# Two half-height PSUM tiles in place of one full-height tile: the first stage of u and the last step of a kernel block

## The chip, the cores and the metric

The kernel runs on one core of one Trainium2 chip. The core has a matmul engine (TensorE, "PE" in the profile, with its weight loads listed as "PEld"), a vector engine (VectorE, DVE), an activation engine (ScalarE, ACT), a general engine (GpSimd, POOL), a queue engine that issues the DMAs (SyncE, SP) and 16 DMA engines. Data lies in SBUF (128 partitions); matmul results go to PSUM, which has eight banks of 128 partitions by 512 float32 numbers. The metric is the time of one execution on the device, in microseconds, smaller being better.

## The reference

Two independent results are put side by side. Left, an S4D state space layer: a long convolution of u with a kernel K made of 256 complex exponentials for each of 448 channels, done with FFTs of twice the length. Right, full softmax attention with 16 heads of 28 over 2048 positions. All numbers are float32.

```python
    def _A_ref(u, log_A_real, A_imag, C_real, C_imag, log_dt, D_skip):
        ...
        A = -jnp.exp(log_A_real) + 1j * A_imag
        C = (C_real + 1j * C_imag) * dt[:, None]
        ...
        P = jnp.exp((A * dt[:, None])[:, :, None] * pos[None, None, :])
        K = 2.0 * jnp.einsum("dn,dnl->dl", C, P).real
        ...
        y = jnp.fft.irfft(Uf * Kf[None, :, :], L2)[:, :, :L]
        ...
        return y + u * D_skip[None, None, :]
    def _B_ref(x, wqkv, wo):
        ...
        scores = jnp.einsum("bhqd,bhkd->bhqk", q, k) * scale
        p = _softmax(scores, axis=-1)
        o = jnp.einsum("bhqk,bhkd->bhqd", p, v)
        return (lambda x, *d: x.transpose(*d))(o, 0, 2, 1, 3).reshape(B, S, D) @ wo
    return jnp.concatenate([a, b], axis=-1)
```

## The kernel before, in words

**The convolution.** The 2048 positions are seen as 32 × 64 (N1 × N2), and each Fourier transform is done as two small matrix products: one of size 32 (cosines and sines of N1, held in the constant `w1`) and one of size 64. For u the first is `u_stage1(q)`, 16 jobs: a job loads 4 × 448 columns of u into one tile `ua` (four channel groups j of 112 channels, 32 rows each, stacked on the 128 partitions). `part(0)` multiplies it by the cosines and `part(1)` by the sines. Each part takes one PSUM tile, issues four matmuls of 32 output columns of the array each (helper `mm32`; the constant is block-diagonal, 128 × 128, so of 128 rows 32 carry numbers for a given output), and lets ScalarE copy the result to half of the tile `ub`. After the second part four DMAs store `ub`. `u_stage2(m)`, 16 more jobs, does the second product.

For the convolution kernel K there are 56 blocks (NB) of eight channels. A block has its powers computed by POOL and DVE (tiles `e` and `g`), and then `k_mm(b)` gives three tasks: `part0(0)` and `part0(1)` multiply e with g and leave `ko`, and `part1` multiplies `ko` by the cosines and sines of `w1`: eight matmuls of 128 columns into one PSUM tile (cosines on partitions 0 to 63, sines on 64 to 127), one ScalarE copy with reordering to `yk`, one DMA. A float32 matmul in the program appears twice in the trace, as two instructions; the matmuls on `fp32r` data of the attention appear once.

**The attention.** It runs in 256 steps (`for s in range(NS)`). A step computes four score tiles (s0 to s3, PSUM tiles `pss`, three buffers), has ScalarE take their exponentials into `p`, and accumulates the product of the step before with v (`po`, four matmuls of 32 output columns). Beside that it computes, for a unit of queries that comes later, the maxima of the scores (m0 to m3): m0 is copied by ScalarE through a Relu into `rl`, m1 is joined with `rl` by a DVE reduction, m2 and m3 are reduced by DVE.

**The order** is written by hand in line 34 and kept on every engine (`nc.kept`, line 864):

```python
ORDER = ('m0', 's0', 'm1', 's1', 'v', 'f', 'pv', 'f', 'v', 'k', 'm2', 's2', 'm3', 's3', 'v')
```

The two `f` are slots, one ahead of `pv` and one behind it. `slot(s)` (line 957) runs in each at most one task: an urgent one (sums of the softmax, ends of the maxima), else a block's task that is due (`m_due`), else a part of u that is due (`u_due`). A new block begins each 3.5 steps (KP), and its three tasks are due in three successive steps; u's jobs come every three steps (UP).

**The ring.** All of m0 to m3 and all tasks in slots take their PSUM tiles from `w_tile()`, which goes round three places (`n_ring[0] % ps_w[1]`, with `ps_w[1]` 3, lines 123 to 128). A tile's first matmul waits until the reader of the tile three before it has finished. PE works in program order, so a matmul that waits holds up all that follow.

The time of each engine's instructions appears under line 75, the helper that records every operation; the tiles' names tell them apart: `pm` is a tile of the ring, `pm<-ua,w` is `part` of `u_stage1`, `pm<-e,g` is `part0`, `pm<-w,ko` is `part1`, `po<-p,v` is `pv`, `pm<-kdif` is m0, other `pm<-khat` are m1 to m3.

Of the kernel before, what the change touches and what calls it, by code (L numbers as in the profile page):

```python
# [8 lines left out]
F32 = mybir.dt.float32  # L9
F32R = mybir.dt.float32r  # L10
I32 = mybir.dt.int32
AF = mybir.ActivationFunctionType
# [6 lines left out]
D = 448  # L19
# [23 lines left out]
K0, KP, KD, UP = 0, 3.5, 4, 3  # L43
# [4 lines left out]
CI = D // 4  # L48
# [42 lines left out]
def body(ctx, tc, a, out):  # L91
    nc = Engines(tc)
    nc.kept = KEPT["p"]
    x, wqkv, wo, u_a = a["B_x"][0], a["B_wqkv"], a["B_wo"], a["A_u"][0]
    out = out[0]

    def pool(stack, name, bufs=1, space=None, side=None):
        kw = {} if space is None else {"space": space}
        if side:
            kw["side"] = side  # L100
        return stack.enter_context(tc.tile_pool(name=name, bufs=bufs, reuse_waits="tile", **kw))
# [6 lines left out]
    yu_d = dram.tile([128, N1, D], F32, name="yu_d")  # L108
# [6 lines left out]
    const = pool(ctx, "const")  # L115
# [1 line left out]
    nc.sync.dma_start(ident, a["ident"])  # L117
    sel = const.tile([128, HG], F32, name="sel")
    kones = const.tile([128, 1], F32, name="kones")
    w1 = const.tile([128, 2, 128], F32, name="w1")  # L120

    att, k0_st = ExitStack(), ExitStack()
    ps_w, n_ring = [None, 3], [0]
# [1 line left out]
    def w_tile():  # L125

        n_ring[0] += 1
        return ps_w[0].tile([128, CQ], F32, name=f"pm{n_ring[0] % ps_w[1]}")
# [7 lines left out]
    def mm32(o, w, x_, start, stop, at=0):  # L136

        for i in range(w.shape[-1] // 32):
            c = slice(32 * i, 32 * i + 32)
            nc.tensor.matmul(o[c], w[:, c], x_, start=start, stop=stop, tile_position=(0, at + 32 * i))  # L140


    kt_g, kd_g, q_u, m_u, mh_u, o_u, rl_u = {}, {}, {}, {}, {}, {}, {}

# [67 lines left out]
    with ExitStack() as st:  # L212
# [47 lines left out]
        t = a["A_log_dt"]  # L260
# [6 lines left out]
        half_pi = s_p.tile([128, 1], F32, name="half_pi")  # L267
        nc.gpsimd.memset(half_pi, TWO_PI / 4)
        nc.sync.dma_start(sel, a["sel"])
        nc.sync.dma_start(w1, a["w1"])  # L270
        for k in range(NCK):
            for s in (1, 0):
                src = wns[k][:, s, :].rearrange("p (g h e) -> p g h e", g=G, e=DH)
# [281 lines left out]
    kq_p = pool(kq_st, "kq_p")  # L555
# [11 lines left out]
    def u_stage1(q):  # L567
        t_ = {}

        def load():  # L570
            u_in = t_["in"] = kq_p.tile([128, 8, CI], F32, name="ua", bufs=2)[:, :4]
            for j in range(4):
                nc.sync.dma_start(u_in[32 * j:32 * j + 32], bass.AP(
                    tensor=u_a.tensor, offset=u_a.offset + 4 * q * D + j * CI, ap=[[N2 * D, 32], [D, 4], [1, CI]]))

        def part(c):
            if c == 0:
                t_["out"] = kq_p.tile([128, 2, 4, CI], F32, name="ub", bufs=2)
            u_in, yt = t_["in"], t_["out"]
            pw = w_tile()  # L580
            mm32(pw[:, :D], w1[:, c, :], u_in.rearrange("p n i -> p (n i)"), start=True, stop=True)
            nc.scalar.activation(yt[:, c].rearrange("p n i -> p (n i)"), pw[:, :D], AF.Copy)
            if c == 1:
                for j in range(4):
                    nc.sync.dma_start(yu_d[8 * q:8 * q + 8, :, j * CI:(j + 1) * CI].rearrange("r k i -> k r i"),
                                      yt[32 * j:32 * j + 32].rearrange("p c n i -> p (c n) i"))
        return [load, lambda: part(0), lambda: part(1)]

    def u_stage2(m):
        t_ = {}  # L590

        def load():
            yu = kq_p.tile([128, 2, D], F32, name="ua", bufs=2)
            mt = kq_p.tile([128, 2, 128], F32, name="mt", bufs=2)
            t_["in"] = yu, mt
            nc.sync.dma_start(yu, yu_d[:, 2 * m:2 * m + 2, :])
            nc.sync.dma_start(mt, a["m2u"][:, 2 * m:2 * m + 2, :])

        def part(c):
            if c == 0:  # L600
                t_["out"] = kq_p.tile([128, 2, 2, DF], F32, name="ub", bufs=2)
            (yu, mt), us = t_["in"], t_["out"]
            pw = w_tile()
            for e in range(2):
                mm32(pw[64 * e:64 * e + 64, :D], mt[:, e, 64 * c:64 * c + 64], yu[:, e, :], True, True, 64 * e)
            for f in range(2):
                nc.scalar.activation(us[:, f, c, :].rearrange("p (b j i) -> p j b i", j=4, i=2),
                                     pw[:, f * DF:(f + 1) * DF].rearrange("p (j b i) -> p j b i", j=4, i=2), AF.Copy)
            if c == 1:
                for f in range(2):  # L610
                    nc.sync.dma_start(uh_d[f][:, m], us[:, f])
        return [load, lambda: part(0), lambda: part(1)]
# [62 lines left out]
    def k_mm(b):  # L675
        t_ = {}

        def part0(i):
            pw = w_tile()
            e, g = egs[b] if i == 0 else egs.pop(b)  # L680
            for n, (h, c) in enumerate(((0, 0), (0, 1), (1, 0), (1, 1))):
                for j in range(4):
                    x_ = h * 8 + i * 4 + j
                    nc.tensor.matmul(pw[32 * j:32 * j + 32, :N2], g[:, c, x_, :], e[:, c, x_, :],
                                     start=n == 0, stop=n == 3, tile_position=(0, 32 * j))
            if i == 0:
                t_["ko"] = g_p.tile([128, 2, N2], F32, name="ko", bufs=2)
            nc.scalar.activation(t_["ko"][:, i], pw[:, :N2], AF.Copy)

        def part1():  # L690
            ko = t_["ko"]
            pw = w_tile()
            for i in range(2):
                for c in range(2):
                    mm32(pw[64 * c:64 * c + 64, i * 128:(i + 1) * 128], ko[:, i, :], w1[:, c, :], True, True, 64 * c)
            yk = g_p.tile([128, N1, 4, 2], F32, name="yk", bufs=2)
            nc.scalar.activation(yk.rearrange("p k j i -> p i j k"),
                                 pw[:, :256].rearrange("p (i j k) -> p i j k", i=2, j=4), AF.Copy)
            nc.sync.dma_start(yk_d[b // NBF][:, :, b % NBF], yk.rearrange("p (m k) j i -> p m (k j i)", k=4))
        return [lambda: part0(0), lambda: part0(1), part1]  # L700

# [174 lines left out]
    u_jobs = [u_stage1(q) for q in range(16)] + [u_stage2(m) for m in range(16)]  # L876

    def u_load(i):
        if i < 32:
            u_jobs[i][0]()  # L880

    def u_part(i, c):
        u_jobs[i][1 + c]()
        if c and i not in (14, 15):
            u_load(i + 2)
        if c and i == 15:
            u_load(16)
            u_load(17)
        if c and i == 31:
            load_wo()  # L890

    u_load(0)
    u_load(1)
    u_due = collections.deque((3 + UP * i + (UP / 2) * c + (4 if i > 15 else 0), i, c) for i in range(32) for c in range(2))
    k_due = collections.deque(range(NB))
    m_due = collections.deque()

# [177 lines left out]
def constants():  # L1075
    import numpy as np
    k = {}
    k["ident"] = np.eye(128)
    sel, ones = np.zeros((128, HG)), np.zeros((128, 1))
    for j in range(HG):  # L1080
        sel[32 * j + DH, j] = 1.0
        ones[32 * j + DH:32 * j + DH + 2] = 1.0
    k["sel"], k["kones"] = sel, ones
    k["pw2"] = np.tile(2.0 ** np.arange(LV), (128, 1))
    n1, k1 = np.arange(N1), np.arange(N1)
    n2, k2 = np.arange(N2), np.arange(N2)
    th = 2 * np.pi * np.outer(n1, k1 + 0.25) / N1
    w1 = np.zeros((2, 128, 128))
    wb = np.zeros((2, 2, N1, 2, N1))
    for j in range(4):  # L1090
        w1[0, 32 * j:32 * j + 32, 32 * j:32 * j + 32] = np.cos(th)
        w1[1, 32 * j:32 * j + 32, 32 * j:32 * j + 32] = np.sin(th)
    for h in range(2):
        wb[h, 0, :, h, :] = np.cos(th).T / L
        wb[h, 1, :, h, :] = np.sin(th).T / L
    k["w1"] = w1.transpose(1, 0, 2)
    k["wb"] = wb.transpose(0, 1, 2, 4, 3).reshape(128, N2)
    ph = 2 * np.pi * ((k1[:, None, None] + 0.25) * n2[None, :, None] / L + n2[None, :, None] * k2[None, None, :] / N2)
    c, s = np.cos(ph).transpose(1, 0, 2), np.sin(ph).transpose(1, 0, 2)
    m2 = np.zeros((2, N2, N1, 2, 64))  # L1100
    m2[0, :, :, 0], m2[0, :, :, 1] = c, s
    m2[1, :, :, 0], m2[1, :, :, 1] = -s, c
    k["m2u"] = m2.reshape(2, 16, 4, N1, 128).transpose(1, 0, 2, 3, 4).reshape(128, N1, 128)
    wa = np.zeros((2, 64, N1, N2, 2))
    ct, st = c.transpose(2, 1, 0), s.transpose(2, 1, 0)
    wa[0, ..., 0], wa[0, ..., 1] = ct, -st
    wa[1, ..., 0], wa[1, ..., 1] = st, ct

    wa = wa.reshape(2, 64, N1, 2, 2, 16, 2).transpose(0, 1, 2, 5, 4, 3, 6)
    k["mw"] = np.concatenate([m2.reshape(128, N1, 128), wa.reshape(128, N1, 128)], -1)  # L1110
    return {n: v.astype(np.float32) for n, v in k.items()}
# [18 lines left out]
```

## Time and profile before

| | us |
|---|---|
| three runs, median (lowest to highest) | 1304.37 (1303.61 to 1306.14) |
| span of the profiled execution, first to last instruction | 1301.1 |
| PE busy in the span | 1228.2 |
| ACT busy | 952.4 |
| DVE busy | 948.0 |
| POOL busy | 871.1 |
| matmuls of `part` of `u_stage1`, 256 instructions, busy | 30.1 |
| matmuls of `part1`, 896 instructions, busy | 36.0 |

The profile gives the profiled execution's span, and no device time of its own beside it; the three runs lie 2.5 to 5.0 us above that span, which is what an execution has ahead of its first and behind its last instruction.

How to read the rows: in the timeline a row has its start and duration in microseconds, the engine, the operation, the tile written and the tiles read, the shape, and how many instructions were merged into it; brackets give the engine's idle time before it and what ended that. In a group's row the numbers behind the bar are busy microseconds, mean nanoseconds of one instruction, and idle time before them with what ended it. For matmuls the duration includes the passage through the array, which overlaps the next matmul: two matmuls in a row show durations that overlap, and the distance of their starts is what each of them costs.

The setup (projections, seeds) fills the first 250 us, the attention steps run from 254 to 1277 us. `u_stage1` runs from 264 to 459 us, `part1` from 275 to 1014 us.

### The profile page before, as it was taken

What the parts mean: (1) busy time and instruction counts of PE and PEld (TensorE: products, weight loads), DVE (VectorE), ACT (ScalarE), POOL (GpSimd) and SP (SyncE); (2) the same over time, 40 slices, a digit from 0 to 9 for tenths busy, and PEclk for the clock granted to TensorE, in tenths of its full rate; (3) what the DMA queues carried; (4) which work ended last, traced back from release to release, by engine and by line L of the source; (5) the groups of instructions that cost most, each with busy time, mean ns of one, the idle gap of its engine ahead of it and who ended that gap; (6) DMA issues with size and microseconds to landing.
All of it is one profiled execution on the core that took longest, in us unless ns stands there. A gap on an engine that the chain in (4) does not pass through costs nothing.

```text
span 1301.1 us, 33177 instructions
## 1 busy us (share of the span) xinstructions
PE 1228.2 (94%) x12625; PEld 701.0 (54%) x12625; DVE 948.0 (73%) x2106; ACT 952.4 (73%) x2068; POOL 871.1 (67%) x736
## 2 busy tenths in 40 slices
PE   6878985899999999999999999999999999999997
PEld 5657763355555555555555555555555555544433
DVE  5887896987777887787788888888888655645111
ACT  4775763488888888888888888888887766756552
POOL 3676683298888878888869999998996212424421
PEclk9888997999999999999999999999999999999999
DMA  6677769835866555458644131733425453647656
GB/s 194 203 258 244 249 206 294 237 77 124 195 137 149 124 146 148 140 147 231 181 126 96 54 95 32 182 91 83 103 51 148 153 158 133 201 144 244 198 162 174
DMA packets 200088, 205.35 MB, mean 158 GB/s; under 512 B 95993, under 2 KB 158521, under 8 KB 197881
## 3 DMA queue, kind: packets, MB, share of 16 engines
q1 hardware_dynamic: 199928, 203.23, 56.2%
q8 instruction: 100, 1.64, 0.5%
q14 instruction: 60, 0.48, 0.1%
HBM read 120.73 MB, written 82.18 MB: 156 GB/s over the span
## 4 chain that ended last, share of the span: by engine, by line
PE 71%; DVE 10%; DMA 6%; POOL 5%; ACT 3%; issue 3%; SPq 0%; POOLq 0%; ACTq 0%; DVEq 0%
PE pm L75 40%; PE pss L75 16%; PE po L75 15%; DVE tri L75 2%; DVE mx L75 2%; POOL e L75 1%; POOL qhat L75 1%; DMA k<-hl 1%; ACT tri L75 1%; DVE qhat L75 1%; DVE sg L75 1%; DMA tri<-in_B_wqkv 1%; DVE px L75 1%; DMA khat<-k 1%; DMA ut<-in_A_u 1%
## 5 line engine op out<-in xcount | busy, mean ns | idle before, releaser
L75 ACT ACTIVATE p<-pss 128x512 f32<-128x512 f32 x1024 | 560.9, 609 | 111.6 <-PE pss L75 108.6
L75 PE MATMUL pss<-qhat,khat 128*128 128x512 f32 x1024 | 402.5, 399 | 1.5 <-ACT p L75 1.4
L75 DVE TENSOR_REDUCE mx<-pm 128x1 f32<-128x512 f32 x500 | 321.4, 684 | 109.2 <-PE pm L75 107.1
L75 PE MATMUL pm<-khat,qhat 128*128 128x512 f32 x749 | 326.3, 438 | 3.4 <-DVE mx L75 2.1
L75 POOL TENSOR_TENSOR e<-e,sdb 128x256 f32<-128x256 f32 x168 | 202.0, 1202 | 116.2 <-ACT e L75 61.2
L75 PE MATMUL po<-p,v 128*32 128x512 f32 x2048 | 269.1, 594 | 0.0
L75 POOL TENSOR_TENSOR e<-e,eu 128x256 f32<-128x256 f32 x168 | 248.4, 1478 | 13.2
L75 PEld LDWEIGHTS pm<-khat,qhat 128*128 128x128 f32 x749 | 141.0, 189 | 199.7 <-ACT p L75 47.8
L75 DVE CUSTOM_DVE_ANT_0 rl<-pm,rl 128x512 f32<-128x512 f32 x249 | 171.4, 688 | 65.2 <-ACT rl L75 61.5
L75 PEld LDWEIGHTS pss<-qhat,khat 128*128 128x128 f32 x1024 | 190.2, 188 | 45.7 <-issue 10.8
L75 POOL TENSOR_TENSOR eu<-e,sdb 128x256 f32<-128x256 f32 x168 | 202.2, 1203 | 0.0
L75 POOL TENSOR_TENSOR p<-pr,pr 64x448 f32<-64x448 f32 x64 | 73.3, 1145 | 158.5 <-PE pm L75 133.2
L75 ACT ACTIVATE rl<-pm 128x512 f32<-128x512 f32 x249 | 150.8, 606 | 20.4 <-PE pm L75 20.4
L75 DVE TENSOR_TENSOR g<-g,zg 128x128 f32<-128x128 f32 x392 | 162.1, 413 | 3.4
L75 PE MATMUL pm<-xh,khat 112*128 112x512 f32 x256 | 94.1, 451 | 23.2 <-DVE hl L75 11.1
L75 PE MATMUL pm<-kdif,qhat 128*128 128x512 f32 x249 | 100.5, 404 | 2.6 <-DMA v<-v 1.3
L75 DVE TENSOR_TENSOR zg<-g,zg 128x128 f32<-128x128 f32 x224 | 88.0, 393 | 5.0
L75 PEld LDWEIGHTS pm<-e,g 128*32 128x32 f32 x3584 | 57.2, 109 | 43.8 <-issue 16.1
L75 DVE TENSOR_TENSOR pr<-pm,ub 128x448 f32<-128x448 f32 x64 | 37.0, 619 | 56.4 <-PE pm L75 42.0
L75 PEld LDWEIGHTS pm<-xh,khat 112*128 112x128 f32 x256 | 54.2, 217 | 39.4 <-DVE hl L75 12.9
L75 PE MATMUL pm<-e,g 128*32 128x64 f32 x3584 | 73.0, 222 | 1.9 <-POOL e L75 1.9
L75 ACT ACTIVATE y<-pm 128x448 f32<-128x448 f32 x48 | 26.5, 553 | 58.2 <-PE pm L75 33.8
(134 smaller groups left out, 1470.3 us busy)
## 6 DMA issues: line engine op xcount, KB each, us to landing
sdb<-sd SPq DMA_DIRECT2D x56, 336.0 KB
khat<-k SPq DMA_DIRECT2D x64, 256.0 KB
qhat<-q SPq DMA_DIRECT2D x64, 256.0 KB
sd<-sg SPq DMA_DIRECT2D x8, 1456.0 KB
k<-hl SPq DMA_DIRECT2D x16, 512.0 KB
q<-hl SPq DMA_DIRECT2D x16, 512.0 KB
mw<-in_mw SPq DMA_DIRECT2D x16, 512.0 KB
sd<-qhat SPq DMA_DIRECT2D x8, 896.0 KB
```

Source lines behind the costliest of these rows:

```text
L75: i = f(*args, **kw)
```

## The change

The constant `w1` (128 × 2 × 128, cosines and sines apart, four blocks on the diagonal) becomes `w2` (128 × 128): rows 0 to 63 and rows 64 to 127 hold the same thing, two blocks of cosines in columns 0 to 63 and two blocks of sines in columns 64 to 127.

`u_stage1` has one task, `both`, in place of two parts. It takes two tiles of the ring at once. Rows 0 to 63 of `ua` (two channel groups) go to the first, rows 64 to 127 to the second, with cosines on the output partitions 0 to 63 and sines on 64 to 127. Its eight matmuls use 64 rows and 32 columns of the array each; the row half changes from one matmul to the next. Two ScalarE copies follow, then four DMAs of the same size as before. `u_due` holds one entry for these jobs, the later of the former two.

`part1` takes two tiles as well and issues 16 matmuls of 64 rows, 32 array columns and 64 moving columns in place of eight of 128 rows and 128 moving columns; the row half is the innermost loop. Two ScalarE copies of 128 numbers per partition replace one of 256.

```diff
-    w1 = const.tile([128, 2, 128], F32, name="w1")
+    w2 = const.tile([128, 128], F32, name="w2")
...
+    def mm64(os, w, x_, start=True, stop=True):
+
+        for i in range(w(0).shape[-1] // 32):
+            c = slice(32 * i, 32 * i + 32)
+            for r, o in enumerate(os):
+                nc.tensor.matmul(o[c], w(r)[:, c], x_(r), start=start, stop=stop, tile_position=(64 * r, 32 * i))
+
+    half = [slice(0, 64), slice(64, 128)]
...
-        def part(c):
-            if c == 0:
-                t_["out"] = kq_p.tile([128, 2, 4, CI], F32, name="ub", bufs=2)
-            u_in, yt = t_["in"], t_["out"]
-            pw = w_tile()
-            mm32(pw[:, :D], w1[:, c, :], u_in.rearrange("p n i -> p (n i)"), start=True, stop=True)
-            nc.scalar.activation(yt[:, c].rearrange("p n i -> p (n i)"), pw[:, :D], AF.Copy)
-            if c == 1:
-                for j in range(4):
-                    nc.sync.dma_start(yu_d[8 * q:8 * q + 8, :, j * CI:(j + 1) * CI].rearrange("r k i -> k r i"),
-                                      yt[32 * j:32 * j + 32].rearrange("p c n i -> p (c n) i"))
-        return [load, lambda: part(0), lambda: part(1)]
+        def both():
+            yt = kq_p.tile([128, 2, 4, CI], F32, name="ub", bufs=2)
+            u_in = t_["in"].rearrange("p n i -> p (n i)")
+            pw = [w_tile() for _ in range(2)]
+            mm64([t[:, :D] for t in pw], lambda r: w2[half[r]], lambda r: u_in[half[r]])
+            for r in range(2):
+                nc.scalar.activation(yt[:, r].rearrange("p n i -> p (n i)"), pw[r][:, :D], AF.Copy)
+            for c in range(2):
+                for j in range(2):
+                    nc.sync.dma_start(yu_d[8 * q + 4 * c:8 * q + 4 * c + 4].rearrange("n k (r j i) -> j k r n i", r=2, j=2)[j],
+                                      yt[64 * c + 32 * j:64 * c + 32 * j + 32])
+        return [load, both]
...
-            pw = w_tile()
+            pw = [w_tile() for _ in range(2)]
             for i in range(2):
                 for c in range(2):
-                    mm32(pw[64 * c:64 * c + 64, i * 128:(i + 1) * 128], ko[:, i, :], w1[:, c, :], True, True, 64 * c)
+                    for j in range(2):
+                        for r in range(2):
+                            n = 64 * c + 32 * j
+                            nc.tensor.matmul(pw[r][n:n + 32, 64 * i:64 * i + 64], ko[half[r], i, 32 * j:32 * j + 32],
+                                             w2[half[r], 64 * c:64 * c + 64], start=True, stop=True, tile_position=(64 * r, n))
             yk = g_p.tile([128, N1, 4, 2], F32, name="yk", bufs=2)
-            nc.scalar.activation(yk.rearrange("p k j i -> p i j k"),
-                                 pw[:, :256].rearrange("p (i j k) -> p i j k", i=2, j=4), AF.Copy)
+            for r in range(2):
+                nc.scalar.activation(yk[:, :, 2 * r:2 * r + 2].rearrange("p k j i -> p i j k"),
+                                     pw[r][:, :128].rearrange("p (i j k) -> p i j k", i=2, j=2), AF.Copy)
...
-        u_jobs[i][1 + c]()
+        u_jobs[i][1 + c if i > 15 else 1]()
...
-    u_due = collections.deque((3 + UP * i + (UP / 2) * c + (4 if i > 15 else 0), i, c) for i in range(32) for c in range(2))
+    u_due = collections.deque((3 + UP * i + (UP / 2) * c + (4 if i > 15 else 0), i, c) for i in range(32) for c in range(2) if i > 15 or c)
```

More of the change, by code (lines that the diff above doesn't have):

```diff
@@ L269, in body @@
         nc.sync.dma_start(sel, a["sel"])
-        nc.sync.dma_start(w1, a["w1"])
+        nc.sync.dma_start(w2, a["w2"])
         for k in range(NCK):
@@ L1087, in constants @@
     th = 2 * np.pi * np.outer(n1, k1 + 0.25) / N1
-    w1 = np.zeros((2, 128, 128))
+    w2 = np.zeros((2, 64, 2, 64))
     wb = np.zeros((2, 2, N1, 2, N1))
-    for j in range(4):
-        w1[0, 32 * j:32 * j + 32, 32 * j:32 * j + 32] = np.cos(th)
-        w1[1, 32 * j:32 * j + 32, 32 * j:32 * j + 32] = np.sin(th)
+    for j in range(2):
+        w2[:, 32 * j:32 * j + 32, 0, 32 * j:32 * j + 32] = np.cos(th)
+        w2[:, 32 * j:32 * j + 32, 1, 32 * j:32 * j + 32] = np.sin(th)
     for h in range(2):
@@ L1095, in constants @@
         wb[h, 1, :, h, :] = np.sin(th).T / L
-    k["w1"] = w1.transpose(1, 0, 2)
+    k["w2"] = w2.reshape(128, 128)
     k["wb"] = wb.transpose(0, 1, 2, 4, 3).reshape(128, N2)
```

## The prediction

> **What bounds the kernel now.** I read the page first: busy times, then the chain that ended last.
>
> ```profile
> span 1301.1 us, 33177 instructions
> PE 1228.2 (94%) x12625; PEld 701.0 (54%) x12625; DVE 948.0 (73%) x2106; ACT 952.4 (73%) x2068; POOL 871.1 (67%) x736
> PE 71%; DVE 10%; DMA 6%; POOL 5%; ACT 3%; issue 3%; SPq 0%; POOLq 0%; ACTq 0%; DVEq 0%
> ```
>
> TensorE holds 71% of the chain. A mean hides stages, so next comes busy time by stretch. The columns are the stretch, its length, then PE, PEld, DVE, ACT, POOL, the granted clock, DMA.
>
> ```profile
> 300.00:400.00 100.00, 99.58 (x1187) 54.30 (x1180) 78.11 (x188) 82.41 (x185) 82.69 (x64) 1.00 0.71 160
> 700.00:800.00 100.00, 99.73 (x1225) 57.22 (x1217) 87.45 (x208) 85.30 (x194) 96.63 (x79) 1.00 0.32 77
> ```
>
> Both edited steps lie between 264 and 1015 us, where PE is over 99% busy at a full clock, ACT some 84%, POOL up to 97%. A matmul's end is modelled, so I go by starts. The timeline shows one attention step and what follows (start, duration).
>
> ```profile
> 343.28 0.39 PE L75 MATMUL pss<-qhat,khat 128*128 128x512 f32 x1
> 343.60 0.65 PE L75 MATMUL pm<-e,g 128*32 128x64 f32 x32
> 344.07 1.04 PE L75 MATMUL po<-p,v 128*32 128x512 f32 x8
> 344.93 0.94 PE L75 MATMUL pm<-ua,w 128*32 128x448 f32 x8
> 345.79 0.50 PE L75 MATMUL pm<-khat,qhat 128*128 128x512 f32 x1
> 346.13 0.40 PE L75 MATMUL pss<-qhat,khat 128*128 128x512 f32 x1
> 346.37 0.39 PE L75 MATMUL pm<-khat,qhat 128*128 128x512 f32 x1
> 346.59 0.40 PE L75 MATMUL pss<-qhat,khat 128*128 128x512 f32 x1
> ...
> 352.61 1.04 PE L75 MATMUL po<-p,v 128*32 128x512 f32 x8
> 353.58 0.50 PE L75 MATMUL pm<-khat,qhat 128*128 128x512 f32 x1
> ```
>
> Starts follow each other at 0.23 us for full-array matmuls and 0.86 us for the eight po, with no hole. So whatever PE gains or loses in a step moves the end by the same amount; nothing later has slack to hide it. Two prices come from here. From the full array into 32-column tiles takes 0.32 (343.28 to 343.60) where the usual distance is 0.23 to 0.24 (346.13 to 346.37): **a change of tile shape costs 0.09 us**. A part of u behind po costs (344.93 − 344.07) + (345.79 − 344.93) − (353.58 − 352.61) = 0.86 + 0.86 − 0.97 = 0.75 us.
>
> **Part 1: the u stage.** A job now has two parts of four column tiles, each in its own slot: 2 × 0.75 = 1.50 us. New: one part, eight tiles of 64 × 32. Each of the instructions still streams 448 columns, and there are as many as in the two old parts together; if the eight tiles run side by side as the four do, one 0.75 remains. Against this stand two new prices.
>
> First, po uses 128-row tiles and u would use 64-row ones, so PE changes shape between them. No row shows 128×32 to 64×32, but the setup has a change in rows alone, from 128 to 64 (the transposes of 56 rows):
>
> ```profile
> 29.58 0.40 PE L75 MATMUL pm<-xl,khat 112*128 112x512 f32 x1
> 29.91 0.71 PE L75 MATMUL pn<-ident,nat 56*128 56x56 f32 x8
> ```
>
> 0.33 us again instead of 0.23: a change in rows costs 0.10. I take 0.10, plus 0.02 for the first weight load that can't run ahead (my estimate: the 0.34 from 345.79 to 346.13 shows a larger one, 0.11, for 128 columns); the bounds are 0 and 0.21. The Trainium skill ("TensorEngine Tiling (Array Packing)", Tiling Modes, Key Properties) says that changing the tiling mode, not just the tile, drains the TensorE. The two rows agree; by this rule the sum is the one below, and without it about 7 us less.
>
> Second, the ring of three PSUM tiles. In order, w_tile serves m0, m1, the two slots, m2, m3. A u job in the slot behind po takes two tiles, so m3 must wait for the eviction of its first.
>
> ```profile
> 345.93 0.55 ACT L75 ACTIVATE ub<-pm 128x448 f32<-128x448 f32 x1 [0.88 <-PE pm L75]
> 348.27 0.69 DVE L75 CUSTOM_DVE_ANT_0 rl<-pm,rl 128x512 f32<-128x512 f32 x1 [0.33 <-ACT rl L75]
> 349.22 0.94 PE L75 MATMUL pm<-ua,w 128*32 128x448 f32 x8
> ```
>
> The eviction starts 0.14 after m2 (345.79) and ends at 0.69; with 0.03 for the signal m3 could start 0.72 after m2, where it now starts at 0.58 (346.37): 0.14 of waiting, and s3, which is behind m3 in PE's queue, waits along. The job's own second tile is that of m1; its reader ends at 348.96, before 349.22: free. So a job costs 0.75 + 0.12 + 0.14 = 1.01, and saves 0.49. From due steps 5, 8, 11, ... and a block's tasks in six of every seven steps I count 14 of 16 behind po (7 us) and two ahead of it. Those meet the wait of part 2 and save about 0.3 each. **u: −7.5 us**; bounds −12 (nothing but halving: 16 × 0.75) and +4 (no halving, 16 × 0.26 of new prices).
>
> **Part 2: the last step of a block, 56 times.** It issues 16 matmul instructions of 128 columns now, 32 of 64 columns then. Here is the first slot, ahead of po, where 49 of the 56 lie: the first, one amid u, and the last, each with the ACT relu of m0.
>
> ```profile
> 274.89 0.61 ACT L75 ACTIVATE rl<-pm 128x512 f32<-128x512 f32 x1
> ...
> 275.11 0.64 PE L75 MATMUL pm<-w,ko 128*32 128x128 f32 x16
> ...
> 347.63 0.61 ACT L75 ACTIVATE rl<-pm 128x512 f32<-128x512 f32 x1
> 347.90 0.65 PE L75 MATMUL pm<-w,ko 128*32 128x128 f32 x16
> 348.11 1.11 ACT L75 ACTIVATE p<-pss 128x512 f32<-128x512 f32 x2
> 348.36 1.04 PE L75 MATMUL po<-p,v 128*32 128x512 f32 x8
> 349.06 0.70 ACT L75 ACTIVATE yk<-pm 128x256 f32<-128x256 f32 x1
> ...
> 1013.30 0.60 ACT L75 ACTIVATE rl<-pm 128x512 f32<-128x512 f32 x1
> ...
> 1013.56 0.65 PE L75 MATMUL pm<-w,ko 128*32 128x128 f32 x16
> 1014.02 1.04 PE L75 MATMUL po<-p,v 128*32 128x512 f32 x8
> ```
>
> The step takes 0.46 us of PE (347.90 to 348.36, 1013.56 to 1014.02). With one tile it takes the ring's place of the previous step's m3, long read. **With two, the second is the place of m0, whose reader is that relu.** It ends at 275.50, 348.24 and 1013.90: 0.39, 0.34 and 0.34 after the step's first matmul. Since the order is r inside j, already the second matmul writes the second tile; it waits, and behind it on PE the 30 others, po and all that follows wait too. ACT can't come earlier: it works through the exponentials of s2 and s3 first. So the wait is some 0.35 + 0.03 = 0.38.
>
> Then come the rest. How fast can PE issue 32? Rows with 32 matmuls in one slot are e,g above (64 columns, four tiles: 0.47) and the sums of 4 columns:
>
> ```profile
> 318.58 0.44 PE L75 MATMUL pm<-sel,o 128*32 128x4 f32 x32
> 318.86 1.06 PE L75 MATMUL po<-p,v 128*32 128x512 f32 x8
> ```
>
> So 32 need at least 0.28 whatever their width, while eight tiles would halve 0.47 to 0.24. I take 0.28; the upper bound is 0.47. Add 0.10 for the change of shape to po. The new slot is 0.38 + 0.28 + 0.10 = 0.76 against 0.46: +0.30, times 49 = **+14.7 us**. The seven behind po have no wait: 0.28 + 0.10 − 0.46 = −0.08, −0.6 us in all. Bounds for this part: −4.5 (56 × −0.08, no wait) and +27 (49 × (0.38 + 0.47 + 0.10 − 0.46) + 7 × 0.11 = 25, and 2 for a longer relu).
>
> The eviction is cut in two:
>
> ```profile
> L75 ACT ACTIVATE yk<-pm 128x256 f32<-128x256 f32 x56 | 39.4, 703 | 3.9 <-PE pm L75 3.9
> L75 ACT ACTIVATE ko<-pm 128x64 f32<-128x64 f32 x112 | 29.1, 259 | 8.3 <-PE pm L75 8.3
> ```
>
> Between 259 ns for 64 columns and 703 for 256, 128 come to 407 by a straight line; two are 0.81 us, 0.11 more (bounds −0.18 and +0.70), 6 us of ACT in all. I cost it at nothing: it follows the exponentials of s0 and s1 (348.11 + 1.11) and ends about 349.9, while ACT then idles up to 0.88 us (the row of ub) and the ring needs the tiles only at m3 and the next m0. Without that cover it would be those 6 us.
>
> Edits with no cost: DMAs on SP's queue stay four per u job, of the same 448-byte rows, and wait for the same last eviction; the constant is half as large and loaded in the setup; POOL issues nothing new. Fewer u slots change no other job's place, since a block's tasks are taken first.
>
> **The sum**: −7.5 + 14.7 − 0.6 = +6.6 us. The span of 1301.1 becomes 1307.7. The runs' median, 1304.37, lies 3.3 above the span; kept, this gives 1311.0.
>
> **Rivals.**
> (a) *Faster: the relu wait is absent or short.* Gain 7.5 + 56 × 0.08 = 12, so 1292. For it: the first matmul needs only the old tile, and some ring orders are free. It decides at a wait under about 0.2 us (49 × (w − 0.08) = 8). Against it: 0.34 to 0.39 in the rows above. 7%.
> (b) *Rows change shape for nothing.* 72 jobs × 0.10 = 7 less: 1304, no change. Against it: the 0.33 of the transposes. 14%.
> (c) *The two row halves don't run side by side*, so the edit doesn't do what it says. u loses 4 instead of gaining 7.5, the block's step costs 25: 1304.4 + 29 = 1333. No row shows two row tiles at once. 9%.
> (d) *ACT becomes late*: the doubled evictions push the next exponentials and relu by about 0.2 us per block and PE waits: 56 × 0.2 = 11 more, 1322. ACT's 85% speaks for it, its idle time against. 8%.
> (e) *A floor per matmul at narrow widths.* At 25 ns each, 32 take 0.8 us, 0.52 over my 0.28: 56 × 0.52 = 29 more, 1340. The row of e,g with 15 ns each (0.47/32) speaks against it. 2%. The Trainium skill ("TensorE: Matmul & The Clock Gate", Back-to-back issue gap) gives about 60 cycles, a 25 ns floor, for widths up to 64; the e,g row does not bear that out for tiles side by side.
>
> **How the numbers follow.** The forecast has 60%, 1311, own range 1306 to 1316. I reach down to (b) and up to (d): 1302.5 to 1323 leaves out (a), (c), (e), 18%. About 0.2% (2.6 us) is what this measurement can tell from no change. Faster: (a) and a share of (b), 11%. Same, 1301.8 to 1307: the rest of (b) and the low edge of the forecast, 17%. Slower: 72%.
>
> **What would show it.** In the timeline after: a hole of about 0.38 us inside the block's step ahead of po, ended by ACT rl; po some 0.76 after that step's first matmul instead of 0.46; u once per job, 0.75 long, with eight tiles starting together; m3 behind it late by 0.14; mean of yk near 407 ns. The forecast is wrong if the first two are absent, or if matmuls of the two halves start one after the other.

## The result

The changed kernel takes 1318.59 us in the median (1316.57 to 1321.71, four runs); the kernel before, beside it, 1303.99 (1303.24 to 1306.14). The ratio is 1.0111, with a 95% interval from 1.0093 to 1.0128: it is slower by about 14.6 us. The profiled execution took 1319.18 us at a span of 1317.2.

The page after, in the lines that answer to those shown of before (span, busy times, chain):

```profile
span 1317.2 us, 35044 instructions
PE 1237.0 (94%) x13521; PEld 693.4 (53%) x13521; DVE 951.1 (72%) x2106; ACT 951.1 (72%) x2124; POOL 870.5 (66%) x736
PE 66%; DVE 13%; ACT 9%; POOL 5%; issue 4%; DMA 3%; SPq 0%; ACTq 0%; POOLq 0%; DVEq 0%
```

PE's share of the chain fell from 71 to 66%, ACT's rose from 3 to 9%: PE now waits for ACT somewhere. The stretches (same columns as before: length, PE, PEld, DVE, ACT, POOL, clock, DMA) say that PE has more idle time in both:

```profile
300.00:400.00 100.00, 97.96 (x1324) 50.34 (x1323) 78.72 (x188) 82.13 (x193) 81.54 (x64) 1.00 0.69 159
700.00:800.00 100.00, 98.79 (x1336) 55.82 (x1339) 86.20 (x205) 83.09 (x196) 94.64 (x75) 1.00 0.31 75
```

PE was at 99.58 and 99.73 there. Now one attention step with a job of u behind po, and the step after it with the block's last task ahead of po, from the timeline of PE after (the two rows below it are weight loads in the same step with u):

```profile
345.28 1.04 PE L75 MATMUL po<-p,v 128*32 128x512 f32 x8
346.25 0.98 PE L75 MATMUL pm<-ua,w 64*32 64x448 f32 x16
347.16 0.50 PE L75 MATMUL pm<-khat,qhat 128*128 128x512 f32 x1
347.50 0.40 PE L75 MATMUL pss<-qhat,khat 128*128 128x512 f32 x1
347.92 0.50 PE L75 MATMUL pm<-khat,qhat 128*128 128x512 f32 x1
348.26 0.39 PE L75 MATMUL pss<-qhat,khat 128*128 128x512 f32 x1
348.49 0.39 PE L75 MATMUL pm<-kdif,qhat 128*128 128x512 f32 x1
...
349.58 0.30 PE L75 MATMUL pm<-w,ko 64*32 64x64 f32 x2
350.12 0.45 PE L75 MATMUL pm<-w,ko 64*32 64x64 f32 x30 [0.25 <-ACT rl L75]
350.50 1.06 PE L75 MATMUL po<-p,v 128*32 128x512 f32 x8
351.50 0.50 PE L75 MATMUL pm<-khat,qhat 128*128 128x512 f32 x1
```

```profile
347.92 0.19 PEld L75 LDWEIGHTS pm<-khat,qhat 128*128 128x128 f32 x1 [0.46 <-ACT ub L75]
348.03 0.19 PEld L75 LDWEIGHTS pss<-qhat,khat 128*128 128x128 f32 x1
```

In the block's step two instructions go out (one matmul, twice in the trace), and the other 30 follow 0.54 us later, released by ACT rl: the hole. po follows 0.38 us after that. u's 16 instructions take 0.91 us (346.25 to 347.16) where eight took 0.86: two parts in little more than the time of one. Behind them m3 starts 0.42 after s2 (347.50 to 347.92), where it was 0.24 (346.13 to 346.37); its weight load has waited for ACT's copy of u (`ub`), and s3 follows only 0.34 after m3.

What the whole attention gained or lost is read from the row of the score matmuls, by the start of its first and its last (durations ns, then both starts, in us). Before:

```profile
L75 PE MATMUL pss<-qhat,khat x1024: 387/396/505, 254.0 to 1275.7; 128*128 128x512 f32 x171
```

After:

```profile
L75 PE MATMUL pss<-qhat,khat x1024: 387/396/628, 255.6 to 1291.9; 128*128 128x512 f32 x171
```

1021.7 us became 1036.3: the 14.6 us lie between these two matmuls. The span grew by 16.1; the other 1.5 us are in the setup of this one execution. Between executions of the same setup the first of these starts differs by up to some 4 us (251.5 to 255.9 over the runs below), so the stage's length is the sharper measure, where the trace of one execution is compared.

### The profile page after: what moved, and what is told of

Same layout as the page of the kernel before. It is cut to its first block, busy times and chain, and to the rows that moved or that the text cites. A ratio compares the mean times of both kernels' runs of the same rounds, so it can differ in the third digit from the quotient of the medians.

```text
span 1317.2 us, 35044 instructions
## 1 busy us (share of the span) xinstructions
PE 1237.0 (94%) x13521; PEld 693.4 (53%) x13521; DVE 951.1 (72%) x2106; ACT 951.1 (72%) x2124; POOL 870.5 (66%) x736
## 4 chain that ended last, share of the span: by engine, by line
PE 66%; DVE 13%; ACT 9%; POOL 5%; issue 4%; DMA 3%; SPq 0%; ACTq 0%; POOLq 0%; DVEq 0%
PE pm L75 37%; PE po L75 15%; PE pss L75 13%; ACT rl L75 3%; ACT p L75 3%; DVE mx L75 3%; DVE tri L75 2%; DVE rl L75 2%; POOL qhat L75 1%; POOL e L75 1%; DVE qhat L75 1%; ACT tri L75 1%; DVE g L75 1%; DVE sg L75 1%; DVE px L75 1%
```

## The experiments

Three theories. **W**: the loss is waiting for a place in the PSUM ring, since two tiles are taken where one was: the block's second tile waits for the relu of m0, and m3 waits for the copy of u's first tile. **S**: the 64-row tiles cost, by their change of shape and by issue at small width. **E**: the eviction cut in two costs ACT time that PE waits for.

### One part at a time

The first two runs did u alone and the block's step alone, with both constants in place:

```diff
     w2 = const.tile([128, 128], F32, name="w2")
+    w1 = const.tile([128, 2, 128], F32, name="w1")
...
         nc.sync.dma_start(w2, a["w2"])
+        nc.sync.dma_start(w1, a["w1"])
```

> The u stage is changed, the block's last step is as before. Theory W (the time goes into waits for a place of the PSUM ring: the relu of m0 inside the block's step, the copy of u's first tile ahead of m3): PE loses 9.3 us of matmul starts by u's halving and gets back 4 us of waiting at m3, so about 1299, and the block's step has its 0.46 us as before. Rival S (the 64-row tiles themselves are what costs, by their change of shape and slow issue): u is hit as well, 1304 to 1308. Rival E (the split eviction on ACT costs): 1295 to 1299, since no eviction of u is split.

> The block's last step is changed, u is as before. W: 49 steps ahead of po lengthen by 0.37 us and seven behind it by 0.15, so 1304 + 19 = 1323, above the changed kernel. S and E: also slower, 1310 to 1323; this run says how much of the loss is this step's, not why.

u alone: 1305.98 (ratio 1.0015, 1.0002 to 1.0027), not the 1299 expected. The block's step alone: 1325.1 (1.0176, 1.0156 to 1.0196), near the 1323 expected. But the attention of the first begins at 258.6 us and that of the second at 261.7, later than anywhere else; the additional constant, loaded in the setup, is in both. So I did the two again with the old constant alone, whose diagonal blocks hold both shapes:

```diff
-                    nc.tensor.matmul(pw[r][n:n + 32, 64 * i:64 * i + 64], ko[half[r], i, 32 * j:32 * j + 32],
-                                     w2[half[r], 64 * c:64 * c + 64], start=True, stop=True, tile_position=(64 * r, n))
+                    nc.tensor.matmul(pw[r][n:n + 32, 64 * i:64 * i + 64], ko[half[r], i, 32 * j:32 * j + 32],
+                                     w1[half[r], c, 64 * r:64 * r + 64], start=True, stop=True, tile_position=(64 * r, n))
```

> u alone once more, now with the old constant alone (its diagonal blocks hold both shapes), so that the setup is that of the kernel before; the earlier run loaded two constants and its attention began 4.6 us later. W: from the trace of the earlier run the steps gain 3.7 us, so about 1300.5. If the loss lies in u's stage itself and not in the setup: 1304 to 1306.

> The block's last step alone, with the old constant alone. W: 18.3 us of PE starts from the trace of the earlier run, so 1322.5; with the u run the two parts add up to the whole (-3.7 + 18.3 = 14.6).

u alone: 1300.57, ratio 0.9967 (0.9954 to 0.9979). The block's step alone: 1320.0, ratio 1.0114 (1.0091 to 1.0138). The score rows of the two, in this order:

```profile
L75 PE MATMUL pss<-qhat,khat x1024: 387/396/628, 251.5 to 1271.3; 128*128 128x512 f32 x171
```

```profile
L75 PE MATMUL pss<-qhat,khat x1024: 387/396/505, 253.9 to 1293.2; 128*128 128x512 f32 x171
```

The attention takes 1019.8 and 1039.3 us: 1.9 less and 17.6 more than before. (In the two runs with both constants it was 3.6 less and 18.3 more, so one execution tells this to some 2 us.) Together 15.7, against 14.6 for the whole change: the parts add up within that, and the loss is the block's step alone. Its 1320.0 is 2.5 below what I expected of it.

### The wait taken away

The changed kernel, with the second tile of the block's step taken from the three places of the score tiles. The place it gets is that of s3 of the step before, whose exponential ACT does ahead of the relu. All else stays: 64 rows, the changes of shape, the split eviction.

```diff
-            pw = [w_tile() for _ in range(2)]
+            pw = [w_tile(), ps_s.tile([128, CQ], F32, name="pss")]
```

> The changed kernel, but the second tile of the block's step comes from the three places of the score tiles (its reader, the exponential of s3, has ended by then), so the wait for the relu is gone while the 64-row tiles, the change of shape and the split eviction stay. W: 49 x 0.41 us go, 1318.6 - 20 = 1298.5, and po starts about 0.40 us after the step's first matmul. S: 1316 to 1319. E: 1312 to 1319.

1297.89 us, ratio 0.9959 (0.9945 to 0.9974) to the kernel before: 20.7 us less than the changed kernel, as W said, and faster than the kernel before. The same place in the timeline of PE, the tiles now alternating between `pm` and `pss`:

```profile
345.62 0.45 PE L75 MATMUL pss<-qhat,khat 128*128 128x512 f32 x1
346.01 0.24 PE L75 MATMUL pm<-w,ko 64*32 64x64 f32 x1
346.06 0.24 PE L75 MATMUL pss<-w,ko 64*32 64x64 f32 x1
...
346.30 0.22 PE L75 MATMUL pss<-w,ko 64*32 64x64 f32 x1
346.44 1.06 PE L75 MATMUL po<-p,v 128*32 128x512 f32 x8
```

The second tile's matmul comes 0.05 us after the first, not 0.54, and po 0.43 after the first. S and E both fall: what they blame is all still there.

The changed kernel has a control of its own. In three of the 49 steps ahead of po the relu has already ended when the block's step begins (rows of PE, and the relu on ACT):

```profile
503.46 0.46 PE L75 MATMUL pm<-w,ko 64*32 64x64 f32 x32
503.84 1.06 PE L75 MATMUL po<-p,v 128*32 128x512 f32 x8
```

```profile
502.72 0.60 ACT L75 ACTIVATE rl<-pm 128x512 f32<-128x512 f32 x1
```

The relu ends at 503.32, there is no hole, and po starts 0.38 after the step's first matmul, less than the 0.46 before.

The counterpart keeps the wait and leaves the 64 rows out: the kernel before, with two tiles of the ring and 16 matmuls of all 128 rows.

```diff
-            pw = w_tile()
+            pw = [w_tile() for _ in range(2)]
...
+                            nc.tensor.matmul(pw[r][n:n + 32, 64 * i:64 * i + 64], ko[:, i, 32 * j:32 * j + 32],
+                                             w1[:, c, 64 * r:64 * r + 64], start=True, stop=True, tile_position=(0, n))
```

> The kernel before, but the block's step writes two tiles of the ring by 16 matmuls of all 128 rows (no 64-row tiles, no change of shape): 32 instructions at 64 columns, as in e,g. W: the wait for the relu is there as with 64 rows (first matmul to po 0.36 + 0.05 + 0.47 = 0.88 us instead of 0.46), 49 x 0.42 = 20.6, so about 1325. S (64-row tiles cost): 1304 to 1308.

1324.37 us, ratio 1.0148 (1.0127 to 1.017). The loss is there without any 64-row tile, and so is the wait, in the weight loads of the step:

```profile
349.30 0.14 PEld L75 LDWEIGHTS pm<-w,ko 128*32 128x32 f32 x2 [0.34 <-DVE mx L75]
349.75 0.41 PEld L75 LDWEIGHTS pm<-w,ko 128*32 128x32 f32 x24 [0.31 <-ACT rl L75]
```

The loss is 4 us larger than that of the 64-row step. That fits 32 instructions on four tiles, not on eight (0.47 us for e,g, 0.38 for the 30 above), but no run separates it. And the eviction by itself, the kernel before with its one copy cut in two:

```diff
-            nc.scalar.activation(yk.rearrange("p k j i -> p i j k"),
-                                 pw[:, :256].rearrange("p (i j k) -> p i j k", i=2, j=4), AF.Copy)
+            for r in range(2):
+                nc.scalar.activation(yk[:, :, 2 * r:2 * r + 2].rearrange("p k j i -> p i j k"),
+                                     pw[:, :256].rearrange("p (i j k) -> p i j k", i=2, j=4)[:, :, 2 * r:2 * r + 2], AF.Copy)
```

> The kernel before, with the block's one eviction cut in two as in the changed kernel, matmuls and tile as before. W: hidden in ACT's idle time, 1303 to 1306. E: 56 x 0.2 = 11 us slower, 1315.

1306.13 us, ratio 1.0008 (0.9996 to 1.0021): no difference that can be told, and at most some 3 us of the 15. The two halves take 483 ns each in the median, where the whole took 704:

```profile
L75 ACT ACTIVATE yk<-pm x112: 398/483/567, 277.8 to 1017.6; 128x128 f32<-128x128 f32 x112
```

### The wait of u

u's second tile from the score places as well, so that m3 does not wait for a copy of u:

```diff
         def both():
...
-            pw = [w_tile() for _ in range(2)]
+            pw = [w_tile(), ps_s.tile([128, CQ], F32, name="pss")]
```

> As the run before, and u's second tile also from the places of the score tiles, so that m3 no longer waits for a copy of u. W: 4 us less than that run, about 1294.5, and m3's matmul starts 0.23 us after s2's in the steps with u. S and E: no difference to it beyond 1 us.

1297.26 us, ratio 0.9954 (0.9937 to 0.9971): the same as without it (0.9959), not the 1294.5 expected. The step behind a job of u: PE first, then the weight load that waited, then ACT:

```profile
345.83 0.50 PE L75 MATMUL pm<-khat,qhat 128*128 128x512 f32 x1
346.16 0.39 PE L75 MATMUL pss<-qhat,khat 128*128 128x512 f32 x1
346.39 0.40 PE L75 MATMUL pm<-khat,qhat 128*128 128x512 f32 x1
...
347.36 0.39 PE L75 MATMUL pm<-khat,qhat 128*128 128x512 f32 x1
347.81 0.51 PE L75 MATMUL pss<-qhat,khat 128*128 128x512 f32 x1
```

```profile
347.81 0.19 PEld L75 LDWEIGHTS pss<-qhat,khat 128*128 128x128 f32 x1 [0.49 <-ACT p L75]
```

```profile
345.99 0.54 ACT L75 ACTIVATE ub<-pm 128x448 f32<-128x448 f32 x1 [1.09 <-PE pss L75]
346.43 0.54 ACT L75 ACTIVATE ub<-pss 128x448 f32<-128x448 f32 x1
346.85 0.42 ACT L75 ACTIVATE e<-sdb 128x256 f32<-128x256 f32 x1
347.16 1.09 ACT L75 ACTIVATE p<-pss 128x512 f32<-128x512 f32 x2
```

m3 is back at 0.23 behind s2 (346.16 to 346.39), as expected; but s1 of the next step now starts 0.45 behind m1, released by ACT p. u's tile stands in the score tiles' ring, so s1 takes the place of s2 and waits for its exponential, which ACT does behind two copies of u and a seed of a block (`e`). The wait has moved. The same with the block's step as before and the old constant:

> u alone, old constant, second tile from the places of the score tiles; the block's step as before. If the wait at m3 only moves (in the run with both steps on score places, m1 and s1 of the next step waited instead, for the exponential of s2 behind the two copies): 1299 to 1301, as u alone with the ring. If that was the block's doing: 1296 to 1297.

1299.63 us, ratio 0.9959 (0.9946 to 0.9972), where the ring's place gave 0.9967 (0.9954 to 0.9979): again no difference, as expected of a wait that only moves, so the block's step is not what took it back. Last, both steps on score places and u's second copy on DVE:

```diff
-            for r in range(2):
-                nc.scalar.activation(yt[:, r].rearrange("p n i -> p (n i)"), pw[r][:, :D], AF.Copy)
+            nc.scalar.activation(yt[:, 0].rearrange("p n i -> p (n i)"), pw[0][:, :D], AF.Copy)
+            nc.vector.tensor_copy(yt[:, 1].rearrange("p n i -> p (n i)"), pw[1][:, :D])
```

> Both steps on score places, and the copy of u's second tile on DVE instead of ACT, so that the exponentials of s2 and s3 come 0.42 us sooner behind a job of u. If ACT's lateness is what took back the wait at m3: 14 x 0.2 = 3 us less than with both copies on ACT, about 1294.5. If not, or if DVE becomes late in its place: 1297 to 1299.

1296.12 us, ratio 0.9941 (0.9925 to 0.9958): the lowest median of all, 8 us below the kernel before and between the two times that I had expected (1294.5, or 1297 to 1299). Its interval overlaps those of the run with both copies on ACT and of the run with the block's tile alone on score places (0.9959), so it is not shown to be faster than either. Its timeline behind a job of u shows where the rest went:

```profile
344.19 0.62 DVE L75 COPY ub<-pss 128x448 f32<-128x448 f32 x1 [0.87 <-PE pss L75]
...
345.06 1.28 DVE L75 TENSOR_REDUCE mx<-pm 128x1 f32<-128x512 f32 x2
...
345.25 0.39 PE L75 MATMUL pss<-qhat,khat 128*128 128x512 f32 x1
...
345.80 0.50 PE L75 MATMUL pm<-khat,qhat 128*128 128x512 f32 x1 [0.16 <-DVE mx L75]
```

The copy pushes DVE's reductions back, the reduction of m2 starts only at 345.06, and m1 of the next step, which takes m2's place, starts 0.55 after s0. A job of u leaves two tiles to empty in a step that has little time to spare on either engine; whichever does it, PE meets the delay in another place.

## Why the prediction was right or wrong

Right were the direction, the place and the mechanism: the block's step waits for the relu of m0 (shown by the run that gives its tile another place), the change of shape is paid, the eight tiles run side by side, and the split eviction costs nothing that can be told, though its halves take 486 ns in the mean of the changed kernel and not 407. Wrong was the size, +6.6 us in the sum and +14.6 measured, and it was wrong in every term.

What each term measured is the sum over its own steps, each from its first score matmul to that of the next step, less the same steps before, in the runs with one part alone:

| term | forecast | measured, two runs each |
|---|---|---|
| 30 steps with a part of u, before or after | −7.5 | −4.9 and −4.7 |
| 49 steps with the block's step ahead of po | +14.7 | +16.7 and +16.9 |
| seven with it behind po | −0.6 | +1.6 and +1.5 |

With u and the seven the step that failed is the same: the wait for a place behind po was put too low (0.14 with u) or at nothing (in the seven), and what it drags along was left out. Ahead of po the wait and the start of po behind it were sized too short. The three add up to about 13.6; another 0.8 is what the two parts do to each other, below.

The measured time lies inside the range of 1302.5 to 1323, but that is luck: it lies above the forecast's own 1316, in the part that was there for rival (d), which is only a small part of the loss. (A device time is 2.0 us above the span of its own execution, 1319.18 to 1317.2, and not 3.3; both sides carry it, so the +6.6 does not depend on it.)

**The block's step, 49 times ahead of po: +0.30 each, 14.7.** First matmul to po was put at 0.76; it is 0.93 in the first case, 0.79 in the last, and 0.80 in the mean of all 49 of the changed kernel.

```profile
276.58 0.30 PE L75 MATMUL pm<-w,ko 64*32 64x64 f32 x2
277.13 0.45 PE L75 MATMUL pm<-w,ko 64*32 64x64 f32 x30 [0.25 <-ACT rl L75]
277.51 1.06 PE L75 MATMUL po<-p,v 128*32 128x512 f32 x8
278.51 0.50 PE L75 MATMUL pm<-khat,qhat 128*128 128x512 f32 x1
...
1028.98 0.85 PE L75 MATMUL pm<-w,ko 64*32 64x64 f32 x32
1029.77 1.06 PE L75 MATMUL po<-p,v 128*32 128x512 f32 x8
```

The part behind the wait was right: 0.28 + 0.10 = 0.38, measured 0.38 (277.13 to 277.51). The wait was taken from three rows, the relu's end 0.34 to 0.39 after the first matmul, and a signal of 0.03. Here the signal takes 0.05 (in the step of the result the relu ends at 350.07, and the 30 start at 350.12). In 14 of the 49 steps ACT does two copies to `ub`, from either stage of u, ahead of the exponentials; there the relu ends 0.46 to 0.50 after the first matmul, the wait is up to 0.55, and po comes after 0.90 to 0.93. In 32 it comes after 0.77 to 0.80, and three have no wait. Eight of the 14 are behind a job of u, whose two copies now stand one after the other: with the block's step alone ACT does one copy there, and po comes after 0.83. That 0.10, eight times, is the 0.8 us that the two parts cost together and neither alone. po itself takes 1.00 to the next matmul instead of 0.97, which fits first weights that are not loaded ahead over a change of shape. So 0.80 + 0.03 − 0.46 = 0.37, times 49 = 18, of which 0.8 is that interplay.

**The seven behind po: −0.08 each, −0.6.** I priced only PE's time there. In four of the seven m3 gets the same wait as with u, and it was not in the sum:

```profile
321.45 0.40 PE L75 MATMUL pss<-qhat,khat 128*128 128x512 f32 x1
322.07 0.50 PE L75 MATMUL pm<-khat,qhat 128*128 128x512 f32 x1 [0.22 <-ACT yk L75]
```

0.62 in place of 0.23 here and in two more, 0.34 in a fourth; in the other three there is no wait. The sentence that the ring "needs the tiles only at m3 and the next m0", by which the longer eviction came to nothing, holds ahead of po and fails behind it. For the block's step, ahead of po and behind it, I forecast +14.1; the attention of the clean run with this step alone is 17.6 longer.

**u: −7.5.** This is the term furthest off. The halving is nearly as forecast: a job behind po takes 346.25 − 345.28 + 347.16 − 346.25 − 0.97 = 0.91 instead of 1.50, where I had 0.87. The wait of m3 was put at 0.14 and is 0.19, and a second price was missed: **a matmul that has waited also holds up the weights of the next one**. The weights of s3 are loaded only 0.11 behind those of m3 (347.92 and 348.03 in the rows of the result), and s3 starts 0.34 after m3 and not 0.23, 0.11 more; I had quoted that 0.34 for a change of shape and not applied it to a wait. 1.50 − 0.91 − 0.30 = 0.29 per job and not 0.49, 4 us for 14; with the two ahead of po, 4.7 to 4.9. The attention's length gave only −1.9 in the clean run and −3.6 in the other because it also holds the steps without u, which differ by +3.0 and +1.0 in these single executions. The runs say −2.7 to −6.0 us by their interval (1304.89 × 0.0021 and × 0.0046), which has the 4.8 inside and the 7.5 outside.

**The change of shape.** Priced at 0.10 from a change in rows elsewhere. It shows in the distance from po to u's first matmul, 0.97 (345.28 to 346.25) where it was 0.86: 0.11. The Trainium skill ("TensorEngine Tiling (Array Packing)", Tiling Modes, Key Properties) has tiles that work independently and a drain at a change of mode, and this trace agrees with both: 16 instructions in 0.91 us where eight took 0.86, and the 0.11.

The rivals: (c), halves that do not run side by side, and (e), a floor of 25 ns per matmul, are refuted by the same rows: 30 instructions and a change of shape in 0.38 us. (b), free changes of shape, by the 0.11. (a), no wait, did not come about, but the run that makes it true gave 1297.9, not the 1292 that I had put to it, mainly because u brought less. (d), ACT being late, I had at 8%; it is a small part of the truth, the 0.8 us above and the moved waits of u, and the split eviction is not what makes it late.

The Trainium skill says in the same page (Restrictions and Gotchas, PSUM Pressure) that row tiling increases PSUM pressure, because different row tiles write to different banks. That is what this change runs into: here the price was 20 us for one further place in a ring of three, while the matmuls themselves took less time than before. Its advice on the PSUM bottleneck (Performance Considerations) to use ScalarE and VectorE both for the copies was tried for u: 1296.12 against 1297.26, intervals overlapping.

## What to carry to other kernels

When an edit takes two places of a ring where it took one, write down for each whose place it gets and when that reader ends, in the very slot where it will run; here the one line that chose the second tile's place decided between 1.1% slower and 0.4% faster. Price a wait on an in-order engine with what it drags behind it: the instruction's wait, the weights of the next that could not be loaded meanwhile, and the readers that come late in the following step. On an engine that is 99% busy, half the array time saved is worth having only if the tiles can be emptied as fast.

## What was not expected

One more constant of 64 KB in the setup cost about 5 us: u alone took 1305.98 with two constants and 1300.57 with one, the block's step alone 1325.1 and 1320.0. The first difference is in the projections. With two constants PE waits 4.1 us, with one 1.0 us (first row with two, second row with one):

```profile
35.51 1.22 PE L75 MATMUL pm<-xh,khat 112*128 112x512 f32 x2 [4.13 <-DVE kb L75]
```

```profile
31.94 0.73 PE L75 MATMUL pm<-xh,khat 112*128 112x512 f32 x2 [0.98 <-DVE kb L75]
```

SyncE's queue issues the loads and stores of the setup in one order, and a load more shifts what they meet; how that makes 5 us of a load of 64 KB I have not followed up, and it stays open.
